# Window attention on one core: nine column pairs with nine tiles off ScalarE, and column heads staged in 128-channel tiles

## The chip, the cores and the metric

The kernel runs on one core of a Trainium2 chip. Each engine of the core takes its instructions in order: PE (TensorE) multiplies matrices into PSUM, ACT (ScalarE) computes exponentials, DVE (VectorE) and POOL (GpSimd) do elementwise work, and SP issues DMAs. The metric is the time of one execution on the device in microseconds (us). "Span" is the time between the first and the last instruction that the profiler saw.

## The reference

The input x is an image of 224 x 224 tokens with C = 96 channels. Half of the heads' channels (C2 = 48) attends within horizontal stripes of 8 rows, the other half within vertical stripes of 8 columns. A stripe has 8 x 224 = 1792 tokens.

```
qkv = einsum('bhwc,cd->bhwd', x, wqkv);  q, k, v = the three thirds
qh, kh, vh = the first 48 channels, as 28 row stripes of 1792 tokens
oh = softmax(qh @ kh^T * 48**-0.5) @ vh
qv, kv, vv = the last 48 channels, as 28 column stripes of 1792 tokens
ov = softmax(qv @ kv^T * 48**-0.5) @ vv
out = einsum('bhwc,cd->bhwd', concat(oh, ov), wo)
```

So there are 56 attention problems of 1792 x 1792 scores with 48 channels, and two projections around them. The row stripes give the first 48 channels of the concatenation ("row heads"), the column stripes the last 48 ("column heads").

## The kernel before, in words

**Pairs and tiles.** Two stripes are computed together as a pair P. Pairs 0 to 13 are row stripes, pairs 14 to 27 are column stripes (`ph_of`, L378; `NPH` is 14, `NP` is 28). The 1792 queries of a pair are cut into chunks of 512, 512, 512 and 256, the keys into 14 groups of 128. A score tile is 128 keys by 512 queries of both stripes, 128 x 1024 numbers in two PSUM banks; in the last chunk two key groups share a tile. A pair has 49 tiles (14 + 14 + 14 + 7).

**Three ways to an exponential.** Most tiles go to ACT: `qk_fn` (L682, matmuls at L689) fills one of two sets of score banks and `emit_qk` (L857) lets ACT write 2 to the power of the scores into a buffer PT (L859). The other tiles, listed in `KINDS` (L21) for each chunk of a pair, go around ACT as a polynomial on DVE and POOL (`emit_p`, L931, and `mids`, L953). A tile of kind P takes one DVE pass over the scores (L943), three POOL operations (L959, L960, L956), and a second set of scores that a second DVE pass (L948) combines with POOL's result. A tile of kind R has two DVE passes first (L943, L945), one POOL operation (L956) and the same closing pass. Both need their scores computed twice (`s_fn`, L695, matmuls at L702), into the ring of four PSUM banks (`RING`, L249). `KIND_OF` (L43) gives the kind of each pair: pair 0 has eight such tiles, pairs 1 to 13 nine, pairs 14 to 27 eight.

**From tile to output.** `pv_fn` (L708, L715) multiplies each finished tile with the values and adds up a chunk in one bank; `emit_ot` (L874) copies it to OT_sb. A DMA transpose (`turn_ot`, L420) puts tokens on partitions, DVE inverts the sums (`emit_rn`, L899), and POOL scales the rows (`emit_norm`, L909). Row heads are then copied by `keep_oh` (L427) into `cat`, which holds for every column stripe the 96 channels of its tokens; column heads are written into `cat` by POOL itself. When a column pair has both parts, `turn_cat` (L440) turns the pair's blocks of 96 channels with a DMA transpose into `oc_all`, packed without gaps: a block of tokens begins in one 128-row tile and may end in the next. `out_fills` (L623, matmuls at L637) multiplies them with `wo6`, which holds `wo` at the needed row offsets, one or two matmuls to each half of a block; DVE copies the result back into `cat` (L642), and each block of 128 tokens of one stripe is stored by one DMA (`emit_evict`, L879). The last pair is different: its row part goes through `out_fills` early, and at the end `fin_fills` (L585, L602) projects the column part straight from OT_sb, and DVE scales and adds it (L609, L614).

**What sets the order.** PE's order is written out by hand in `ORDER` (L44), one string for each pair. A letter is one step: q scores for ACT, v a PV step, 1 and 3 the first scores of a polynomial tile (in two halves or as one), 2 and 4 its closing scores, k the next of the projections for the following pair (`prep_fills`, L510), g the next head projection, f a step of `fin_fills`. From the letters a planner in the kernel's own program, with set durations for each kind of step, gives DVE, POOL and SP their orders (`dve_step`, `pool_step`, L996 and L1068). On the chip the orders are fixed and semaphores hold each instruction until its inputs are there. SP issues nearly all DMAs in one order: loads, transposes, copies and stores.

## Time and profile before

| | |
|---|---|
| median of 3 runs | 1062.62 us (1061.92 to 1063.65) |
| the profiled execution | 1062.68 us |
| its span | 1060.9 us |
| first exponential of a tile starts | 9.57 us |
| last exponential of a tile ends | 1055.97 us |
| granted PE clock, mean | 0.999 |

The page gives busy shares of each engine, then groups of instructions by source line: how many, their total and mean duration, and the idle time just before them with what ended it. A busy share counts overlapping instructions once. Stretches of the span are compared in a table by stage: pair 0 runs from 9.6 to 47.8 us, pairs 1 to 13 to 526.7, pair 14 to 565.2, pairs 15 to 26 to 1018.2, and pair 27 to 1056.0, each counted from its first exponential.

### The profile page before, as it was taken

What the parts mean: (1) busy time and instruction counts of PE and PEld (TensorE: products, weight loads), DVE (VectorE), ACT (ScalarE), POOL (GpSimd) and SP (SyncE); (2) the same over time, 40 slices, a digit from 0 to 9 for tenths busy, and PEclk for the clock granted to TensorE, in tenths of its full rate; (3) what the DMA queues carried; (4) which work ended last, traced back from release to release, by engine and by line L of the source; (5) the groups of instructions that cost most, each with busy time, mean ns of one, the idle gap of its engine ahead of it and who ended that gap; (6) DMA issues with size and microseconds to landing.
All of it is one profiled execution on the core that took longest, in us unless ns stands there. A gap on an engine that the chain in (4) does not pass through costs nothing.

```text
span 1060.9 us, 33547 instructions
## 1 busy us (share of the span) xinstructions
PE 1033.4 (97%) x13812; PEld 393.5 (37%) x13812; DVE 998.2 (94%) x1720; ACT 1049.3 (99%) x1146; POOL 935.5 (88%) x617
## 2 busy tenths in 40 slices
PE   9999999999999999999999999999999999999998
PEld 4333333333333333333334433333343443344433
DVE  8999999999999999999999999999999999999988
ACT  8999999999999999999999999999999999999998
POOL 7999999999988989999999778888888878979784
PEclk9999999999999999999999999999999999999999
DMA  9987648754963874322115334423332342332342
GB/s 182 160 153 112 100 80 145 112 96 84 144 96 56 139 108 69 38 56 58 40 20 99 76 54 76 88 38 77 80 69 52 81 83 49 79 79 40 64 65 44
DMA packets 376217, 88.58 MB, mean 83 GB/s; under 512 B 366944, under 2 KB 373376, under 8 KB 376064
## 3 DMA queue, kind: packets, MB, share of 16 engines
q1 hardware_dynamic: 374816, 85.85, 46.8%
q8 instruction: 108, 1.77, 0.7%
q10 hardware_dynamic: 1120, 0.49, 0.2%
q14 instruction: 45, 0.37, 0.1%
q0 software_dynamic: 128, 0.10, 0.0%
HBM read 28.36 MB, written 28.21 MB: 53 GB/s over the span
## 4 chain that ended last, share of the span: by engine, by line
PE 54%; ACT 28%; DVE 7%; issue 6%; POOL 4%; DMA 0%; ACTq 0%; POOLq 0%; DVEq 0%
ACT PT L859 28%; PE ps L715 20%; PE ps L689 20%; PE ps L702 7%; PE ps L521 3%; DVE qb L943 2%; DVE PT L948 2%; PE ps L637 2%; POOL PT L959 2%; PE ps L566 1%; POOL PT L956 1%; POOL PT L960 1%; DVE PT L945 1%; DVE KT_sb L526 1%; POOL cat L920 0%
## 5 line engine op out<-in xcount | busy, mean ns | idle before, releaser
L859 ACT ACTIVATE PT<-ps 128x1024 bf16<-128x1024 f32 x1135 | 1044.8, 1087 | 2.8 <-PE ps L689 1.8
L689 PE MATMUL ps<-QT_sb,KT_sb 49*64 49x512 bf16 (+1 forms) x5368 | 465.3, 363 | 17.6 <-ACT PT L859 10.5
L956 POOL TENSOR_TENSOR PT<-PT 128x1024 f16<-128x1024 f16 x237 | 445.1, 1892 | 41.1 <-DVE PT L945 24.1
L715 PE MATMUL ps<-PT,V_sb 128*49 128x512 bf16 (+1 forms) x3136 | 464.7, 362 | 0.3
L948 DVE SCALAR_TENSOR_TENSOR PT<-ps,PT 128x512 uint16<-128x512 f32 (+1 forms) x398 | 302.0, 787 | 20.8 <-PE ps L702 13.5
L943 DVE TENSOR_SCALAR qb<-ps 128x512 f16<-128x512 int16 (+1 forms) x404 | 302.3, 778 | 20.3 <-PE ps L702 15.8
L959 POOL TENSOR_TENSOR PT<-qb 128x1024 f16<-128x1024 f16 x141 | 266.1, 1892 | 54.8 <-DVE qb L943 24.9
L689 PEld LDWEIGHTS ps<-QT_sb,KT_sb 49*64 49x64 bf16 x5368 | 136.4, 103 | 305.8 <-ACT PT L859 280.9
L715 PEld LDWEIGHTS ps<-PT,V_sb 128*49 128x49 bf16 x3136 | 134.8, 103 | 211.1 <-issue 181.4
L702 PE MATMUL ps<-QT_sb,KT_sb 53*64 53x512 bf16 (+1 forms) x1896 | 189.4, 389 | 4.0 <-DVE PT L948 0.7
L960 POOL TENSOR_SCALAR PT<-PT 128x1024 f16<-128x1024 f16 x141 | 147.1, 1043 | 12.0
L945 DVE SCALAR_TENSOR_TENSOR PT<-ps,qb 128x512 f16<-128x512 int16 (+1 forms) x166 | 122.5, 766 | 0.5
L702 PEld LDWEIGHTS ps<-QT_sb,KT_sb 53*64 53x64 bf16 (+1 forms) x1896 | 53.8, 104 | 71.2 <-DVE PT L948 21.7
L876 DVE CAST OT_sb<-ps 113x512 bf16<-113x512 f32 x112 | 69.1, 617 | 3.0 <-PE ps L715 2.7
L535 DVE CAST QT_sb<-ps 128x512 bf16<-128x512 f32 (+1 forms) x111 | 67.2, 616 | 2.5 <-PE ps L521 1.7
L526 DVE TENSOR_SCALAR_CACHE_REDUCE KT_sb<-ps 128x512 bf16<-128x512 f32 x108 | 65.4, 616 | 1.3 <-PE ps L521 0.6
L642 DVE CAST cat<-ps 128x480 bf16<-128x480 f32 x84 | 51.5, 617 | 5.1 <-PE ps L637 4.5
L573 DVE CAST V_sb<-ps 128x480 bf16<-128x480 f32 (+1 forms) x84 | 51.7, 620 | 1.5 <-PE ps L566 1.2
L521 PE MATMUL ps<-xT_sb,w_sb 97*64 97x512 bf16 (+1 forms) x224 | 40.7, 364 | 0.0
L521 PE MATMUL ps<-xT_sb,wq_sb 97*64 97x512 bf16 x224 | 40.5, 366 | 0.1
L637 PE MATMUL ps<-wo,oc_all 128*64 128x96 bf16 x1176 | 39.9, 208 | 0.0
L566 PEld LDWEIGHTS ps<-w_sb,xT_sb 96*64 96x64 bf16 x1568 | 33.1, 112 | 17.7 <-issue 7.4
(64 smaller groups left out, 254.7 us busy)
## 6 DMA issues: line engine op xcount, KB each, us to landing
xT_sb<-xt_dram SPq DMA_DIRECT2D x28, 336.0 KB, 4.0
out_dram<-cat SPq DMA_DIRECT2D x382, 24.0 KB, 1.9
xp_dram<-in_x_dram SPq DMA_DIRECT2D x26, 336.0 KB
oc_all<-xp_dram SPq DMA_DIRECT2D x26, 336.0 KB, 4.4
xt_dram<-xT_sb SPq DMA_DIRECT2D x26, 336.0 KB, 6.4
cat<-ohn SPq DMA_DIRECT2D x52, 84.0 KB, 3.2
xt_dram<-xT_sb SPq DMA_DIRECT2D x4, 168.0 KB, 5.3
OT_tr<-OT_sb SPq DMA_TRANSPOSE x40, 3.4
```

The lines of the kernel that those rows point to most:

```text
L521: ins = e.matmul(bk[64 * w:64 * w + 64, 0:qs], lhsT=lw, rhs=xT_sb[b][0:C + 1, w, q0:q0 + qs], start=True, stop=True)
L526: return e.tensor_scalar(KT_sb[b][:, q0:q0 + qs], bk[:, 0:qs], alpha, None, ALU.mult, ALU.add, accum_out=ksum[b][:, c:c + 1])
L689: ins = e.matmul(bank(SETS[s] + w)[64 * kh:64 * kh + 64, i * t["qs"]:(i + 1) * t["qs"]], lhsT=KT_sb[b][64 * w:64 * w + CA, kt * 128 + 64 * ...
L702: ins = e.matmul(bank(bp[w])[64 * kh:64 * kh + 64, 0:512], lhsT=KT_sb[b][64 * w:64 * w + nr, kt * 128 + 64 * kh:kt * 128 + 64 * kh + 64], ...
L715: ins = e.matmul(bank(pb)[64 * w:64 * w + CA, 0:t["qs"]], lhsT=V_sb[b][:, w, kt, :], rhs=PT[slot][:, ca:ca + t["qs"]], start=st and i == 0 ...
L859: S.commit("act", 0.0, D_ACT, None, lambda e, s=s, slot=slot: e.activation(PT[slot][:], ps[:, 512 * SETS[s]:512 * SETS[s] + 1024], ACTF.Ex ...
L943: fn, reads, writes = lambda e: e.tensor_scalar(q, l, m, a, ALU.mult, ALU.add), bk, qk
L945: fn, reads, writes = lambda e: e.scalar_tensor_tensor(y.bitcast(FP16), l, -RA * 2.0 ** 16, q, ALU.add, ALU.mult), bk + qk, ptk
L948: fn, reads, writes = lambda e: e.scalar_tensor_tensor(y.bitcast(U16), f, 128.0, y.bitcast(FP16), ALU.mult, ALU.add), bk + ptk, ptk
L956: square = ("pool", D_SQ, lambda e: e.tensor_tensor(y, y, y, ALU.mult), yk + ["pser"], yk)
L959: return [("pool", D_SQ, lambda e: e.tensor_tensor(y, q, q, ALU.mult), qk, yk), ("pool", D_AF, lambda e: e.tensor_scalar(y, y, -(QS * (RB ...
L960: ("pool", D_AF, lambda e: e.tensor_scalar(y, y, -(QS * (RB + RA) / 2) ** 2, 1.0, ALU.add, ALU.mult), yk + ["pser"], yk),
```

## The change

- `KINDS` has a fourth kind with nine polynomial tiles (six P, three R), and nine of the column pairs have it: 15, 16, 17, 19, 20, 21, 23, 24 and 25. The other column pairs keep eight.
- Row heads are kept in `oh_all`. For a column pair, `rows_in` copies its row heads from there into one of two staging buffers `stg`, in which every block of tokens has 128 channels, 32 of them unused; POOL writes the column heads into the same buffer, and `turn_cat` turns it. A block of tokens then lies in one 128-row tile. Every half block takes one matmul, with one copy of `wo` in place of six. The copy is issued when the pair's first scores are; for pairs 27 and 14 it is issued in two parts, at the end of pairs 12 and 13's row work.
- The two turns of a pair no longer wait for each other through the old input buffer, and DVE's copies of the projection go into `og` and no longer back into `cat`, so they don't wait for the turns either.
- A block of the projection now holds 128 tokens, every partition two neighbouring ones: the weights are loaded with a step of two elements (`c (t u) -> c u t`), and one store carries two blocks, 384 bytes from each partition.
- The clearing of the unused channels (`stgz`) stands with the first memsets of the kernel; before, two smaller memsets stood in `later`.
- `do_fill2` and `emit_both` let one DVE instruction copy two neighbouring banks of a projection (letters K and G). The new `ORDER` has one K and no G.
- `ORDER` is new for pairs 0 to 4 and 11 to 27, and unchanged for pairs 6 to 10; that of pair 5 begins differently. Some of the planner's durations are new.

```diff
-KINDS = ["PPR PPR PP ", "PPR PRR PPR ", "PPR PPR PR "]
+KINDS = ["PPR PPR PP ", "PPR PRR PPR ", "PPR PPR PR ", "PPR PPR PPR "]
...
+KIND_OF = [0, 1, 1, 1, 1, 1, 1, 1, 1, 1, 1, 1, 1, 1, 2, 3, 3, 3, 2, 3, 3, 3, 2, 3, 3, 3, 2, 2]
 ORDER = [
...
-    "qv1qvvqvvvqgvqv2qvvq1vqgq3vqvkq3qvkqvvqkvvq4vqvkvq2vqgvq2qkvvqvvkq2qgvvq1qvv3qvkqvqvkqv4qgvvq3qvvvvq4qvvgq1qvv2qvqkvqvkkkqqvvv",
...
+    "vv1qvq4vqvkqvkq1vqgvqvvqv4qvvkq2qvvq1vvkqv1qkvq2qvvkqvgvq2qvvgvq1qvvgqvvvqv1qvqkq4gqvgvq3qvkq4qvvgq1qkvqvvkqvqvkgqv2qvq2vqvkvv",
...
-        cat = sb("cat", [128, NPH, NPH, 2, C], BF16)
+        oh_all = sb("oh_all", [128, NPH, NPH, 2, C2], BF16)
+        stg = [sb(f"stg{i}", [128, NKT, 2, 128], BF16) for i in range(2)]
+        og = [sb(f"og{i}", [128, NKT // 2, 2, 2, C], BF16) for i in range(3)]
         OT_tr = [sb(f"OT_tr{i}", [128, NKT, 128], BF16) for i in range(2)]
         ohn = sb("ohn", [128, NKT, 2, C2], BF16)
         rn = [sb(f"rn{i}", [128, 2 * NKT], FP32) for i in range(2)]
-        wo6 = sb("wo6", [128, 6, C], BF16)
-
-        x0_sb = cat[0:TH].rearrange("p a m w c -> p (a m w c)")[:, 0:2 * NTH * C].rearrange(
+        wo6 = sb("wo6", [128, C], BF16)
+
+        x0_sb = oh_all[0:TH].rearrange("p a m w c -> p (a m w c)")[:, 0:2 * NTH * C].rearrange(
             "p (w k c) -> p w k c", w=2, k=NTH)
-        NQT = 2 * NKT * C // 128
+        NQT = 2 * NKT
...
-            pool_now([("cat", NPH - 1)], lambda e: e.memset(cat[:, NPH - 1, :, :, C2:C].rearrange("p m w c -> p (m w) c").bitcast(FP32), 0.0), 0.7)
-            pool_now(["wo6z"], lambda e: e.memset(wo6[:].rearrange("p v c -> p (v c)").bitcast(FP32), 0.0), 0.3)
+        pool_now([("stgz", 0)], lambda e: e.memset(stg[0][:, :, :, C:].rearrange("p m w c -> p (m w) c").bitcast(FP32), 0.0), 0.5)
+        pool_now([("stgz", 1)], lambda e: e.memset(stg[1][:, :, :, :].rearrange("p m w c -> p (m w c)").bitcast(FP32), 0.0), 1.8)
...
-        def turn(semn, reads, writes, out_ap, in_ap):
-            d = {k for k in S.deps("dma", reads, writes) if k[0] != semn}
+        def turn(semn, reads, writes, out_ap, in_ap, old=()):
+            d = {k for k in S.deps("dma", reads, writes + list(old)) if k[0] != semn}
...
-                        dma("sp", [("ohn", 0), ("ohn", 1)], ["oh"], cat[64 * w:64 * w + 64, :, P, s_, 0:C2], src, "nc", tot)
+                        dma("sp", [("ohn", 0), ("ohn", 1)], ["oh"], oh_all[64 * w:64 * w + 64, :, P, s_, :], src, "nc", tot)
+
+        def rows_in(P, m0=0, m1=NPH):
+            b = P % 2
+            dma("sp", ["oh", ("stgz", b)], [("sr", b)], stg[b][:, m0:m1, :, 0:C2].rearrange("p m w c -> p (m w) c"),
+                oh_all[:, P - NPH, m0:m1, :, :].rearrange("p m w c -> p (m w) c"), f"ri{b}")
 
         def turn_cat(P, z):
-            b, a = P % 2, P - NPH
+            b = P % 2
             k0, k1 = ((0, 8), (8, NKT))[z]
-            flat = cat[:, a, :, :, :].rearrange("p m w c -> p (m w c)")
             x_old = [("x", w) for w in range(2)] if P in (NPH, NP - 1) else []
-            turn(f"oc{b}{z}", ["oh", ("cat", a), ("ov", a, z)], [("ocT", b, z), ("catd", a, z)] + x_old,
-                 oc_T[b][:, k0 * 2 * C // 128:k1 * 2 * C // 128, :], flat[:, k0 * 2 * C:k1 * 2 * C])
+            turn(f"oc{b}{z}", [("sr", b), ("sc", b, z), ("stgz", b)], [("ocT", b, z)],
+                 oc_T[b][:, 2 * k0:2 * k1, :], stg[b][:, k0:k1, :, :].rearrange("p m w c -> p (m w c)"), x_old)
 
         def load_wo():
-            for r0, n, p0, v in ((0, 96, 0, 0), (0, 32, 96, 1), (32, 64, 0, 2), (0, 64, 64, 3), (64, 32, 0, 4), (0, 96, 32, 5)):
-                dma("sp", ["wo6z"], ["wo6"], wo6[p0:p0 + n, v, :], wo[r0:r0 + n, :], "w2", 96)
+            dma("sp", [], ["wo6"], wo6[0:C, :], wo[:, :], "w2", 16)
...
-        dst_all = out[0].rearrange("(kt hh) (j dw) c -> j kt hh dw c", hh=16, dw=8)
+        dst_all = out[0].rearrange("(kp hh) (j dw) c -> j kp hh (dw c)", hh=32, dw=8)
...
-                                    t0 = (k0 + s) * 128 + 64 * h
+                                    t0 = (k0 + h) * 128
                                     ins = e.matmul(bk3[64 * h:64 * h + 64, s, :],
-                                                   lhsT=OT_sb[b][64 * w:64 * w + CA, t0:t0 + 64],
+                                                   lhsT=OT_sb[b][64 * w:64 * w + CA, t0:t0 + 128].rearrange("c (t u) -> c u t", u=2)[:, s, :],
...
-                            def d2(e, bk, s=s, ri=ri, w=w, kt=k0 + s, j=j):
+                            def d2(e, bk, s=s, ri=ri, w=w, kp=k0 // 2):
                                 bk3 = bk[:, 0:FS * (C + 1)].rearrange("p (s c) -> p s c", s=FS)
-                                return e.scalar_tensor_tensor(cat[:, NPH - 1, kt, w, :], bk3[:, s, 0:C], rc[ri][:, s:s + 1],
-                                                              cat[:, NPH - 1, kt, w, :], ALU.mult, ALU.add)
+                                return e.scalar_tensor_tensor(og[2][:, kp, w, s, :], bk3[:, s, 0:C], rc[ri][:, s:s + 1],
+                                                              og[2][:, kp, w, s, :], ALU.mult, ALU.add)
                             chain.append((0.225, d2, [("rc", ri), "add"], [("o", P, w, k0 + s)], None,
-                                          [(P, w, k0 + s)]))
+                                          [(P, w, k0 // 2, [("o", P, w, k0 + z) for z in range(n)])] if s == n - 1 else []))
...
-            rows = cat[:, a, :, :, :].rearrange("p m w c -> p (m w) c")
+            rows = og[2 if P == NP - 1 else b][:, :, :, :, :].rearrange("p m w s c -> p (m w s) c")
...
-                        q, r = divmod(3 * (k0 + s), 4)
-                        use = {0: ((0, 0),), 3: ((0, 1), (1, 2)), 2: ((0, 3), (1, 4)), 1: ((0, 5),)}[r]
-                        for i, (dq_, v) in enumerate(use):
-                            for h in range(2):
-                                ins = e.matmul(bk[64 * h:64 * h + 64, s * C:(s + 1) * C], lhsT=oc_T[b][:, q + dq_, 64 * h:64 * h + 64],
-                                               rhs=wo6[:, v, :], start=i == 0, stop=i == len(use) - 1)
+                        m, u = divmod(k0 + s, 2)
+                        for h in range(2):
+                            ins = e.matmul(bk[64 * h:64 * h + 64, s * C:(s + 1) * C],
+                                           lhsT=oc_T[b][0:C, 4 * (m // 2) + 2 * h + m % 2, :].rearrange("c (t u) -> c u t", u=2)[:, u, :],
+                                           rhs=wo6[0:C, :], start=True, stop=True)
                     return ins
 
                 def d(e, bk, k0=k0, n=n):
                     return e.tensor_copy(rows[:, k0:k0 + n, :], bk[:, 0:n * C].rearrange("p (s c) -> p s c", s=n))
                 last = P == NP - 1
-                st = [] if last else [(P, (k0 + s) % 2, (k0 + s) // 2) for s in range(n)]
-                fills.append(fill("B", 0.063 * n, pe_fn, ["wo6"] + [("ocT", b, y) for y in range(z + 1)],
-                                  [(0.07 + 96 * n * 0.001026, d, [("catd", a, y) for y in range(z + 1)], ["add"] if last else [("o", P, k0)], None, st)],
+                st = [] if last else [(P, m % 2, m // 2, sorted({("og", b, 2 * m // FS * FS), ("og", b, k0)})) for m in range(k0 // 2, (k0 + n) // 2)]
+                fills.append(fill("B", D_G * n, pe_fn, ["wo6"] + [("ocT", b, y) for y in range(z + 1)],
+                                  [(0.07 + 96 * n * 0.001026, d, [], ["add"] if last else [("og", b, k0)], None, st)],
...
-                    P, w, kt = item
-                    key = ("o", P, w, kt) if P == NP - 1 else st[3][0]
-                    dma(q, [key], [], dst_all[2 * (P - NPH) + w, kt], cat[:, P - NPH, kt, w, :], "op" if q == "gq" else f"out{P % 2}")
+                    P, w, kp, keys = item
+                    dma(q, keys, [], dst_all[2 * (P - NPH) + w, kp],
+                        og[2 if P == NP - 1 else P % 2][:, kp, w, :, :].rearrange("p s c -> p (s c)"), "op" if q == "gq" else f"out{P % 2}")
+
+        def emit_both(f1, f2, b0, done):
+            g, h = f1["gives"], f2["gives"]
+            P, b = g[1], g[1] % 2
+            if g[0] in "KQ":
+                q0, n = CH_Q0[g[2]], CH_SIZES[g[2]] + CH_SIZES[h[2]]
+                src = ps[:, 512 * b0:512 * b0 + n]
+                if g[0] == "K":
+                    def fn(e):
+                        return e.tensor_scalar(KT_sb[b][:, q0:q0 + n], src, alpha, None, ALU.mult, ALU.add,
+                                               accum_out=ksum[b][:, k_i[P, g[2]]:k_i[P, g[2]] + 1])
+                else:
+                    def fn(e):
+                        return e.tensor_copy(QT_sb[b][:, q0:q0 + n], src)
...
+            sts = [f1["chain"][0], f2["chain"][0]]
+            d = sts[0][0] + sts[1][0] - D_M2
+            S.commit("dve", 0.0, d, d + SEMD, fn, [("bank", b0), ("bank", b0 + 1)] + sorted(set(sts[0][2] + sts[1][2]), key=str), sts[0][3] + sts[1][3])
+            for st in sts:
...
-                    dst = cat[:, P - NPH, k0:k1, :, C2:C].rearrange("p m w c -> p (m w) c")
+                    dst = stg[b][:, k0:k1, :, C2:C].rearrange("p m w c -> p (m w) c")
...
-                            tm["sp"] += 3.5 + 5.3
-                            for y in range(2):
-                                turn_cat(NP - 1, y)
-                                g_t[NP - 1, y] = tm["sp"] + TURN
+                            rows_in(NP - 1, NPH - 1)
+                            rows_in(NPH, NPH - 1)
+                            tm["sp"] += 7.5
+                            turn_cat(NP - 1, 1)
+                            g_t[NP - 1, 1] = tm["sp"] + TURN
+                        elif P == NPH - 2:
+                            rows_in(NP - 1, 0, NPH - 1)
+                            rows_in(NPH, 0, NPH - 1)
+                            tm["sp"] += 10.4
+                            turn_cat(NP - 1, 0)
+                            g_t[NP - 1, 0] = tm["sp"] + TURN
...
-                    tm["sp"] = max(tm["sp"], st) + 1.5
+                    tm["sp"] = max(tm["sp"], st) + (4.0 if P > NPH else 3.2)
+                    if P > NPH:
+                        rows_in(P)
...
-                do_fill(c)
+                do_fill2(c.lower()) if c in "KG" else do_fill(c)
```

132 lines of the change are left out of this document (95 added, 37 removed).

## The prediction

> **What bounds the kernel now.** I read the page's busy shares first, then the costliest groups, then the busy time by stage, then who ACT waited for.
>
> ```profile
> span 1060.9 us, 33547 instructions
> PE 1033.4 (97%) x13812; PEld 393.5 (37%) x13812; DVE 998.2 (94%) x1720; ACT 1049.3 (99%) x1146; POOL 935.5 (88%) x617
> ...
> L859 ACT ACTIVATE PT<-ps 128x1024 bf16<-128x1024 f32 x1135 | 1044.8, 1087 | 2.8 <-PE ps L689 1.8
> ```
>
> Four engines stand above 88%, so a share alone does not say which one is the limit. The group row does: 1135 exponentials fill 1044.8 us with 2.8 us of idle before them.
>
> The next fence is the busy time by stage. Its columns are the stretch, its length, then PE, weight loads, DVE, ACT and POOL with the instructions in brackets. The rows are pair 0, pairs 1 to 13 (row heads, nine tiles each off ACT), two of those pairs on their own, pair 14, pairs 15 to 26 (column heads, eight tiles), and pair 27. Instructions that straddle an edge are counted in both stretches, so I count exponentials by KINDS: 41 where eight of the 49 tiles of a pair go elsewhere, 40 where nine do.
>
> ```profile
> 9.60:47.80 38.20, 36.76 (x522) 13.11 (x520) 36.62 (x66) 38.00 (x41) 34.26 (x22) 1.00 1.02 166
> 47.80:526.70 478.90, 465.84 (x5828) 167.43 (x5824) 461.10 (x774) 478.34 (x522) 446.02 (x293) 1.00 0.58 94
> 195.60:269.40 73.80, 72.01 (x900) 25.30 (x898) 71.98 (x121) 73.78 (x81) 71.90 (x46) 1.00 0.66 108
> 526.70:565.20 38.50, 37.78 (x481) 13.61 (x480) 36.41 (x64) 38.02 (x43) 37.56 (x25) 1.00 0.26 52
> 565.20:1018.20 453.00, 447.33 (x6402) 178.64 (x6400) 423.01 (x703) 452.65 (x493) 384.27 (x239) 1.00 0.36 69
> 1018.20:1056.00 37.80, 36.71 (x514) 14.65 (x510) 33.47 (x78) 37.77 (x42) 25.87 (x19) 1.00 0.27 52
> ```
>
> Per exponential that is 478.90/(13x40) = 0.921 us with row heads and 453.00/(12x41) = 0.921 us with column heads. The spacing is the same whether nine tiles go elsewhere or eight, while POOL's share is 93% in one and 85% in the other. So time is the number of exponentials times 0.921 us, wherever the other engines follow. Two places are slower: pair 14 (0.939 us) and pair 0 (0.932 us).
>
> ```profile
> ACT PT L859 <- PE ps L689: 1.8, 3, 1.2
> ACT PT L859 <- DVE PT L945: 0.3, 1, 0.3
> ```
>
> ACT's own waits come to 2.1 us, so the path is ACT, and PE answers each freed score bank just in time.
>
> **The change, part by part.**
>
> *Nine pairs with nine tiles.* KIND_OF gives kind 3 to nine column pairs, so 9 exponentials go (1135 to 1126, as the letter q counts in the two order lists). On ACT: 9 x 0.921 = 8.3 us less. In their place come nine tiles of kind P on PE, DVE and POOL. The rows are POOL's groups over the whole run, two DVE groups of pairs 15 to 26, and one line of the timeline.
>
> ```profile
> L956 POOL TENSOR_TENSOR PT<-PT 128x1024 f16<-128x1024 f16 x237 | 445.1, 1892 | 41.1 <-DVE PT L945 24.1 <-DVE wq_sb L552 7.5 <-PE ps L715 0.7
> L959 POOL TENSOR_TENSOR PT<-qb 128x1024 f16<-128x1024 f16 x141 | 266.1, 1892 | 54.8 <-DVE qb L943 24.9 <-ACT PT L859 8.9 <-PE ps L702 7.2
> L960 POOL TENSOR_SCALAR PT<-PT 128x1024 f16<-128x1024 f16 x141 | 147.1, 1043 | 12.0
> ...
> L943 DVE TENSOR_SCALAR qb<-ps 128x512 f16<-128x512 int16 x113 | 73.5, 683 | 5.4 <-PE ps L702 4.4
> L943 DVE TENSOR_SCALAR qb<-ps 128x1024 f16<-128x1024 int16 x39 | 47.6, 1221 | 6.2 <-PE ps L702 5.6
> ...
> 1047.07 1.29 DVE L948 SCALAR_TENSOR_TENSOR PT<-ps,PT 128x512 uint16<-128x512 f32 x2 [0.17 <-PE ps L702]
> ```
>
> POOL: 1.892 + 1.043 + 1.892 = 4.83 us a tile, 43.4 us for nine. DVE: two steps of 1.22 us (one wide) to 1.29 us (two halves), so 2.5 us a tile and 22.5 us in all. All nine tiles lie in pairs 15 to 25, so I set them against pairs 15 to 26: those will take (12x41 - 9) x 0.921 = 444.8 us. POOL: 384.27 + 43.4 = 427.7 us, 96%. DVE: 423.01 + 22.5 = 445.5 us, 100% as busy time counts. That overstates DVE, because a second half behind a first costs only 1.29 - 0.68 = 0.61 us, while the 113 halves of the row above fill 73.5 us, 0.65 each; that is 6% to be had by packing, up to 27 us over all of DVE. The two-pair row near 200 us shows that such a load can be carried: DVE 71.98 and POOL 71.90 of 73.80 us, 97% each, and ACT spaced 73.80/80 = 0.9225 us. I charge the nine pairs that spacing: 9 x 40 x 0.0015 = 0.5 us. The bound below is nothing; the bound above is pair 14's 0.939 us, the worst stretch here with POOL at 37.56 of 38.50: 9 x 40 x 0.018 = 6.5 us. I take 0.5, since the long row is the nearer load.
>
> *128-channel tiles for the column heads.* A head's block then needs two matmuls where three were the mean (1176 over 14 pairs x 28 blocks). The rows are the group and two places of the timeline.
>
> ```profile
> L637 PE MATMUL ps<-wo,oc_all 128*64 128x96 bf16 x1176 | 39.9, 208 | 0.0
> ...
> 605.34 0.69 PEld L637 LDWEIGHTS ps<-wo,oc_all 128*64 128x64 bf16 x30 [0.23 <-issue]
> ...
> 1037.66 0.41 PE L702 MATMUL ps<-QT_sb,KT_sb 53*64 53x512 bf16 x4
> 1037.90 0.39 PE L689 MATMUL ps<-QT_sb,KT_sb 49*64 49x512 bf16 x4
> 1038.22 0.49 PE L637 MATMUL ps<-wo,oc_all 128*64 128x96 bf16 x14
> 1038.64 0.41 PE L689 MATMUL ps<-QT_sb,KT_sb 49*64 49x512 bf16 x4
> 1038.98 0.62 PE L715 MATMUL ps<-PT,V_sb 128*49 128x512 bf16 x4
> ```
>
> Thirty weight loads start over 0.69 - 0.11 = 0.58 us, 20 ns each. So 392 matmuls fewer give PE 7.8 us. The last rows are starts on PE: score step to score step 0.24 us, score step to the other mode 0.34 us, so a change of mode costs 0.10. In pairs 14 to 27 the new list has 11 steps more (1760 against 1749) and 47 changes of mode fewer (959 against 1006). PE: -7.8 + 11 x 0.24 - 47 x 0.10 = -9.9 us. None of it is on the path, where ACT sets the pace; it is what makes room for the nine tiles.
>
> The remaining matmuls, and the last pair's at L602, load weights with a step of two elements (c u t). No row shows such a load. From below it costs nothing; from above twice the 20 ns, 784 x 20 = 15.7 us, which would make PE 5.8 us dearer than now. I take nothing, as the row whose count and width it shares. [...] No run here shows a stepped load yet.
>
> *Staging, turns, stores.* These go through SP's queue. The rows are three lines of the DMA issues (the last number is the median time to landing), the issue times of stores and turns on SP (shortest, median, longest ns), the turns' time to landing, and one turn in the timeline.
>
> ```profile
> out_dram<-cat SPq DMA_DIRECT2D x382, 24.0 KB, 1.9
> ...
> cat<-ohn SPq DMA_DIRECT2D x52, 84.0 KB, 3.2
> ...
> cat<-ohn SPq DMA_DIRECT2D x8, 42.0 KB, 2.2
> ...
> L287 SPq DMA_DIRECT2D out_dram<-cat x382: 538/598/1897, 594.5 to 1058.0; - x191
> ...
> L414 SPq DMA_TRANSPOSE oc_all<-cat x28: 1282/1434/2536, 560.3 to 1031.3; - x28
> ...
> DMA to landing us min/median/max: 3.2/4.5/6.0
> ...
> 1031.34 1.39 SPq L414 DMA_TRANSPOSE oc_all<-cat  x1
> ```
>
> Stores: 392 issues become 196. At 0.6 us each SP gains 118 us, or nothing if an issue of two blocks takes twice as long; either way SP is a waiter and no engine waits for a store before the last. rows_in adds one 336 KB copy a pair in 96-byte pieces. The nearest rows are the 84 and 42 KB copies of such pieces: 1.0 us for 42 KB more, so 2.2 + 7 x 1.0 = 9.2 us to landing, and no less than the 3.2 us of a quarter of it. It is issued when the pair's first scores are, ahead of both its turns, and the first turn waits in any case for the pair's first two chunks, 28 of its 49 PV steps: some 20 us. Hidden. A turn carries 16 and 12 tiles for 12 and 9: 1.43 to 1.9 us of issue, landing 4.5 to at most 6.0, or 6.0 to 8.0 if all of it scales. The tightest turn now is issued at 1031.34 and its first matmul starts at 1038.22, 6.9 us later. In the order lists the least distance from the last PV of a chunk to its first G grows from 21 to 23 exponentials for the first part and from 20 to 25 for the second, 1.8 and 4.6 us. So PE does not come to wait; cost nothing.
>
> *Start and end*, from the timeline.
>
> ```profile
> 1.40 1.59 POOL L331 MEMSET xT_sb<- 1x1792 f32 x1 [0.32 <-DVE ident L327]
> ...
> 8.83 0.69 POOL L362 MEMSET wqT<- 128x256 bf16 x2
> 12.81 3.74 POOL L959 TENSOR_TENSOR PT<-qb 128x1024 f16<-128x1024 f16 x2 [3.29 <-DVE qb L943]
> ...
> 1058.53 0.53 POOL L287 DMA_DIRECT2D out_dram<-cat  x1 [2.41 <-DVE cat L614]
> ```
>
> The two memsets of stg now run ahead of POOL's first tile: 1.6 us for 1792 words (stg1) and some 0.5 for a quarter of that. POOL idles 3.29 us there, so they are covered; without that cover they would push POOL's first tiles by 2.1 us, not ACT. At the end the last store is issued at 1058.53, after the last sum, and the span ends 2.4 us later. It still is one store after one sum, so the tail stays. The one paired K eviction saves DVE about 0.06 us.
>
> **The sum.** 1062.68 us is the profiled execution (span 1060.9 and 1.8 around it), 0.06 over the median of 1062.62. 1062.68 - 8.3 + 0.5 = 1054.9 us.
>
> **The rivals.**
>
> *A. The nine tiles overload POOL (slower).* POOL at 427.7 of 444.8 us leaves 17.1 us, 1.4 us a pair, for its waits on DVE and on its own results. The static order makes PE wait at the closing score step of a late tile, and the next scores stand behind that step. In pairs 1 to 13 POOL idled (478.90 - 446.02)/13 = 2.5 us a pair, in the two heavy pairs 0.95. At 2.5 the twelve pairs take 427.7 + 30 = 458 us instead of 444.8, and the run 1054.4 + 13.2 = 1067.6 us. The break-even with before is (444.8 + 8.3 - 427.7)/12 = 2.1 us a pair. For it: POOL's waits on L943 and L945 above. Against: that idleness was had where nothing pressed POOL. DVE at its limit would look the same.
>
> *B. Half of it.* POOL or DVE idles some 1.75 us a pair: 427.7 + 21 = 448.7, 3.9 us over, 1058.3 us.
>
> *C. Stepped weight loads are slow.* PE becomes 5.8 us dearer in a stage where it is busy 447.33 of 453.00 us, so up to 5.8 us go on the path: 1060.2 us. [...]
>
> *D. The order repairs pairs 0 and 14.* Both get new lists. At 0.921 us they would take 37.8 us each, 0.4 and 0.7 us less: 1053.8 us; and down to 1051.5 if spacing falls by 0.002 throughout.
>
> **How the numbers follow.** Forecast 0.60, D 0.12, B 0.10, C 0.07, A 0.11. The range 1051.5 to 1060.5 goes from D's floor to just past C and the worst case of the nine pairs (1054.4 + 6.5 = 1060.9), and leaves out A. A change within 0.2% (2.1 us) is about what a measurement of this kernel cannot tell from none. B and C are still faster by more than that, but C with the 6.5 us on top would be no change. So faster 0.85, same 0.04, slower 0.11.
>
> **What would show it.** Right: 1126 exponentials at 0.921 us or a little over in pairs 15 to 26, POOL and DVE each at 95% or more there, 784 matmuls in the head projection at 20 ns, ACT's waits still near 2 us. Wrong: spacing above 0.935 with the closing score steps waiting for POOL (A), weight loads of the projection above 20 ns apart (C), or PE waiting for a turn.

## The result and the profile after

The changed kernel takes 1056.15 us (median of 6 runs, 1055.85 to 1058.0), the kernel before 1062.34 us in the runs beside them. The ratio is 0.9944, 95% interval 0.9932 to 0.9957. The forecast was 1054.9 us with a range of 1051.5 to 1060.5 and most of the chance on "faster". The profiled execution is one of the longer ones, 1057.54 us with a span of 1055.7; the sum below is made against it.

The head of the page and the row of the exponentials:

```profile
span 1055.7 us, 32757 instructions
PE 1027.3 (97%) x13456; PEld 385.9 (37%) x13456; DVE 1014.0 (96%) x1748; ACT 1041.8 (99%) x1137; POOL 985.1 (93%) x654
...
L867 ACT ACTIVATE PT<-ps 128x1024 bf16<-128x1024 f32 x1126 | 1037.2, 1080 | 4.1 <-PE ps L697 2.9
```

Nine exponentials are gone and 356 matmuls. ACT is still the engine that is never free: 1126 exponentials fill 1037.2 us with 4.1 us of idle before them. The busy time by stage, cut where a pair's first exponential starts, with the columns as before: pair 0, pairs 1 to 13, pair 14, pairs 15 to 26, pair 27.

```profile
10.70:48.30 37.60, 36.67 (x522) 13.15 (x516) 35.82 (x59) 37.58 (x41) 34.54 (x24) 1.00 0.98 175
48.30:527.00 478.70, 465.95 (x5830) 166.04 (x5824) 461.12 (x772) 478.32 (x522) 448.71 (x293) 1.00 0.50 93
527.00:565.70 38.70, 38.52 (x504) 14.53 (x502) 37.72 (x66) 38.24 (x43) 36.92 (x23) 1.00 0.72 83
565.70:1011.90 446.20, 438.33 (x6002) 169.84 (x5998) 434.03 (x735) 445.18 (x485) 421.28 (x264) 1.00 0.51 83
1011.90:1049.80 37.90, 37.51 (x530) 15.81 (x528) 36.92 (x79) 37.87 (x42) 32.84 (x27) 1.00 0.49 81
```

Pairs 15 to 26 went from 453.00 to 446.20 us; every other stage stayed within 0.7 us of its time before. The five stretches together are 7.3 us shorter (1046.4 to 1039.1 us), and 6.8 of these lie there. Per exponential the stage stands at 446.20/483 = 0.924 us (0.921 before).

ACT's own waits for scores (in total, times, longest; the longest stands ahead of the first exponential, so only 0.6 us lie behind it), and the end of the span, from the timeline (start, length, then the instruction; in brackets the idle time before it):

```profile
ACT PT L867 <- PE ps L697: 2.9, 4, 2.3
```

```profile
1051.49 0.97 DVE L623 SCALAR_TENSOR_TENSOR og<-ps,rc,og 128x96 bf16<-128x96 f32 x4
1051.79 0.55 POOL L291 DMA_DIRECT2D out_dram<-og  x1 [0.67 <-DVE og L623]
1052.53 1.09 POOL L291 DMA_DIRECT2D out_dram<-og  x2 [0.19 <-DVE og L623]
```

The last exponential ends at 1049.81, the last sum at 1052.46. Then two stores, each of two blocks, are issued one after the other on POOL's queue, 1.09 us for both. Before, one store followed the last sum. The span ends 5.9 us after the last exponential, 4.9 before.

The new transfers, from the DMA issues (size, then median us to landing) and from the issue times of turns and stores on SP (shortest, median, longest ns). The line of landing times covers all DMAs that read or write `oc_all`; its longest, 7.9, is a turn:

```profile
out_dram<-og SPq DMA_DIRECT2D x181, 48.0 KB, 2.0
...
stg<-oh_all SPq DMA_DIRECT2D x13, 336.0 KB, 6.0
...
oc_all<-stg SPq DMA_TRANSPOSE x28, 4.4
```

```profile
L418 SPq DMA_TRANSPOSE oc_all<-stg x28: 1427/1887/4453, 539.6 to 1035.1; - x28
...
DMA to landing us min/median/max: 3.1/4.0/7.9
```

```profile
L291 SPq DMA_DIRECT2D out_dram<-og x181: 538/601/1592, 594.4 to 1049.9; - x181
```

A store of 384 bytes a partition costs SP the same 0.60 us as one of 192 did (medians), the copy of the row heads lands in 6.0 us and a turn in 4.4, at most 7.9. In pairs 15 to 26 PE waited for no DMA.

### The profile page after: what moved, and what is told of

Its sections match the earlier page's. It is cut to its first block, busy times and chain, and to the rows that moved or that the text cites. A ratio compares the mean times of both kernels' runs of the same rounds, so it can differ in the third digit from the quotient of the medians.

```text
span 1055.7 us, 32757 instructions
## 1 busy us (share of the span) xinstructions
PE 1027.3 (97%) x13456; PEld 385.9 (37%) x13456; DVE 1014.0 (96%) x1748; ACT 1041.8 (99%) x1137; POOL 985.1 (93%) x654
## 4 chain that ended last, share of the span: by engine, by line
PE 54%; ACT 22%; DVE 10%; POOL 7%; issue 6%; DMA 0%; ACTq 0%; POOLq 0%; DVEq 0%
ACT PT L867 22%; PE ps L723 20%; PE ps L697 20%; PE ps L710 7%; DVE PT L994 3%; POOL PT L1002 3%; PE ps L530 3%; DVE qb L989 3%; POOL PT L1005 2%; PE ps L575 1%; POOL PT L1006 1%; PE ps L644 1%; DVE PT L991 1%; DVE og L650 1%; DVE V_sb L582 1%
## 5 line engine op out<-in xcount | busy, mean ns | idle before, releaser
L867 ACT ACTIVATE PT<-ps 128x1024 bf16<-128x1024 f32 x1126 | 1037.2, 1080 | 4.1 <-PE ps L697 2.9
L1002 POOL TENSOR_TENSOR PT<-PT 128x1024 f16<-128x1024 f16 x246 | 461.8, 1894 | 20.3 <-DVE PT L991 11.3
L994 DVE SCALAR_TENSOR_TENSOR PT<-ps,PT 128x512 uint16<-128x512 f32 (+1 forms) x405 | 312.4, 799 | 15.7 <-PE ps L710 6.8
L989 DVE TENSOR_SCALAR qb<-ps 128x512 f16<-128x512 int16 (+1 forms) x421 | 313.7, 775 | 11.9 <-PE ps L710 7.8
L1005 POOL TENSOR_TENSOR PT<-qb 128x1024 f16<-128x1024 f16 x150 | 283.2, 1894 | 22.9 <-DVE qb L989 10.8
L710 PE MATMUL ps<-QT_sb,KT_sb 50*64 50x512 bf16 (+1 forms) x1968 | 196.6, 390 | 5.3 <-DVE PT L994 1.2
L1006 POOL TENSOR_SCALAR PT<-PT 128x1024 f16<-128x1024 f16 x150 | 156.9, 1046 | 12.8
L710 PEld LDWEIGHTS ps<-QT_sb,KT_sb 50*64 50x64 bf16 (+1 forms) x1968 | 55.8, 103 | 76.3 <-DVE PT L994 22.9
L650 DVE CAST og<-ps 128x480 bf16<-128x480 f32 x84 | 51.4, 617 | 1.4 <-PE ps L644 0.7
L530 PE MATMUL ps<-xT_sb,w_sb 97*64 97x512 bf16 x224 | 41.9, 371 | 0.3 <-DVE qb L989 0.2
L575 PE MATMUL ps<-w_sb,xT_sb 96*64 96x48 bf16 x1568 | 39.1, 190 | 0.0
```

The source lines that it names most:

```text
L530: ins = e.matmul(bk[64 * w:64 * w + 64, 0:qs], lhsT=lw, rhs=xT_sb[b][0:C + 1, w, q0:q0 + qs], start=True, stop=True)
L575: ins = e.matmul(bk[64 * h:64 * h + 64, j * C2:(j + 1) * C2], lhsT=xT_sb[b][0:C, w, t0:t0 + 64], rhs=w_sb[0:C, wblk(P, "v"), 0:C2], start= ...
L710: ins = e.matmul(bank(bp[w])[64 * kh:64 * kh + 64, 0:512], lhsT=KT_sb[b][64 * w:64 * w + nr, kt * 128 + 64 * kh:kt * 128 + 64 * kh + 64], ...
L867: S.commit("act", 0.0, D_ACT, None, lambda e, s=s, slot=slot: e.activation(PT[slot][:], ps[:, 512 * SETS[s]:512 * SETS[s] + 1024], ACTF.Ex ...
L989: fn, reads, writes = lambda e: e.tensor_scalar(q, l, m, a, ALU.mult, ALU.add), bk, qk
L994: fn, reads, writes = lambda e: e.scalar_tensor_tensor(y.bitcast(U16), f, 128.0, y.bitcast(FP16), ALU.mult, ALU.add), bk + ptk, ptk
```

## The experiments

Times of stages in this part are worked out from the rows of the exponentials, as in the tables by stage. "Stretch" is the time from the first exponential's start to the last one's end: 1046.4 us before, 1039.1 in the profile after.

### The parts without the nine tiles, and the nine tiles without the parts

The first kernel is the changed one with the lists of the kernel before, the second the kernel before with the new lists (one K written as kk).

```diff
-KINDS = ["PPR PPR PP ", "PPR PRR PPR ", "PPR PPR PR ", "PPR PPR PPR "]
+KINDS = ["PPR PPR PP ", "PPR PRR PPR ", "PPR PPR PR "]
-KIND_OF = [0, 1, 1, 1, 1, 1, 1, 1, 1, 1, 1, 1, 1, 1, 2, 3, 3, 3, 2, 3, 3, 3, 2, 3, 3, 3, 2, 2]
+KIND_OF = [0, 1, 1, 1, 1, 1, 1, 1, 1, 1, 1, 1, 1, 1, 2, 2, 2, 2, 2, 2, 2, 2, 2, 2, 2, 2, 2, 2]
 ORDER = [
...
```

> The changed kernel with the kinds and the order list of before: staging in 128-channel tiles, rows copied ahead, stores of two blocks, but 1135 exponentials. Theory (the time is the number of exponentials times 0.921 us, the other parts only make room): as before, 1061 to 1064 us, ACT spacing 0.921 us, although the head projection has 392 matmuls fewer. Rival (the relief of PE and SP is itself worth the gain): 1056 to 1059 us.

Measured: 1064.28 us, ratio 1.0015 [1.0006, 1.0025], just above the range that was expected. The stage of pairs 15 to 26:

```profile
566.00:1019.90 453.90, 444.10 (x6044) 170.89 (x6042) 422.42 (x703) 452.77 (x493) 384.21 (x239) 1.00 0.53 84
```

It took 453.9 us (453.0 before) and the stretch 1047.0 (1046.4). So staging, free turns, stores of two blocks and two matmuls in place of three bring nothing by themselves, although PE's busy time in the stage fell from 447.3 to 444.1 us.

```diff
-KIND_OF = [0, 1, 1, 1, 1, 1, 1, 1, 1, 1, 1, 1, 1, 1, 2, 2, 2, 2, 2, 2, 2, 2, 2, 2, 2, 2, 2, 2]
+KIND_OF = [0, 1, 1, 1, 1, 1, 1, 1, 1, 1, 1, 1, 1, 1, 2, 3, 3, 3, 2, 3, 3, 3, 2, 3, 3, 3, 2, 2]
 ORDER = [
...
```

> The kernel before with the new kinds and the new order list (its one letter K written as two k): 1126 exponentials, but three matmuls to a block, the old staging and a store for each block. Theory (room on PE is needed for the nine tiles): part of the 8.3 us is lost, 1057 to 1061 us, with spacing in pairs 15 to 26 above 0.924 us. Rival (ACT's count alone decides, PE had room enough): 1055 to 1057 us, as the changed kernel.

Measured: 1072.8 us, ratio 1.0102 [1.0084, 1.012], a loss and outside both expectations. Three prices come out of its trace against that of the changed kernel. Pair 14 took 44.9 us instead of 38.7; its timeline shows why:

```profile
561.66 5.00 SPq L414 DMA_TRANSPOSE oc_all<-cat  x2
...
565.41 0.77 PE L637 MATMUL ps<-wo,oc_all 128*64 128x96 bf16 x14 [4.07 <-DMA oc_all<-cat]
...
567.72 1.02 ACT L859 ACTIVATE PT<-ps 128x1024 bf16<-128x1024 f32 x1 [5.55 <-PE ps L689]
```

The new order asks for the projection of pair 27's row part earlier than before, and without the row heads staged ahead its turn is issued only at 561.66; in the changed kernel that turn goes out at 539.57. PE stands 4.07 us, ACT 5.55, and PE's granted clock is at half from 563.12 to 569.95 us (more of that below). Pairs 15 to 26 took 451.9 us instead of 446.2, though the same tiles were on POOL and DVE:

```profile
571.40:1023.40 452.00, 443.45 (x6344) 175.01 (x6343) 433.87 (x734) 448.75 (x484) 416.88 (x260) 1.00 0.35 66
```

PE has 342 matmuls more in it (6344 against 6002). The run with repeated matmuls below puts a price of 3.4 us on 268; what makes the rest of these 5.7 us isn't shown. And the tail was 9.6 us, with single-block stores still queued:

```profile
1057.74 11.84 SPq L287 DMA_DIRECT2D out_dram<-cat  x17
...
1060.84 7.16 ACTq L287 DMA_DIRECT2D out_dram<-cat  x11
```

So the nine tiles give the gain and the parts make it possible: neither does anything useful alone. This holds for the new lists, which were made for the new parts; lists with nine tiles made for the old parts were not run.

### Is the rest POOL's, DVE's or PE's?

The stage ended 0.9 us above the forecast of 445.3. Three kernels take work away from an engine by leaving out columns of the polynomial tiles. One more kernel adds work to PE.

POOL: the affine step on half of the columns.

```diff
-lambda e: e.tensor_scalar(y, y, -(QS * (RB + RA) / 2) ** 2, 1.0, ALU.add, ALU.mult)
+lambda e: e.tensor_scalar(y[:, 0:512], y[:, 0:512], -(QS * (RB + RA) / 2) ** 2, 1.0, ALU.add, ALU.mult)
```

> The changed kernel, with POOL's middle operation on half of its columns (left out: the affine step on the other half of each polynomial tile of kind P), all orders unchanged: POOL has about 0.5 us less in each of 150 tiles. If POOL's lateness makes the stalls of the nine-tile pairs (rival A of the prediction): ACT's stretch from first to last exponential falls from 1039 to 1036 us or less. If not: it stays within 1 us of 1039.

Measured: 1055.67 us, ratio 0.9935 [0.992, 0.995]. POOL's work in pairs 15 to 26 fell from 421.3 to 392.5 us, the stage took 446.3 us and the stretch 1038.8.

```profile
563.60:1009.90 446.30, 438.17 (x6002) 169.59 (x5998) 433.26 (x734) 445.27 (x485) 392.45 (x263) 1.00 0.51 83
```

Nothing came of 28.8 us less, so POOL's lateness makes none of the remaining stalls.

DVE: the closing pass on half of its columns.

```diff
+                if h == 2:
+                    f, y = f[:, :, 0:256], y[:, :, 0:256]
+                else:
+                    f, y = f[:, 0:256], y[:, 0:256]
                 fn, reads, writes = lambda e: e.scalar_tensor_tensor(
```

> The changed kernel, with DVE's closing pass on half of its columns (left out: the exponent of the other half), all orders unchanged: DVE has about 0.5 us less in each of 246 tiles. If DVE's lateness makes the stalls: ACT's stretch falls from 1039 to 1035 us or less, near 1126 x 0.917 = 1032.5. If not: it stays within 1 us of 1039.

Measured: 1055.19 us, ratio 0.9929 [0.9912, 0.9946]; the stage 445.5, the stretch 1037.5. 46.4 us less work on DVE (434.0 to 387.6) bought 0.7 us in the stage and 1.6 in the stretch, between the two outcomes that were expected.

PE and DVE: that kernel with the closing scores on half of their columns too.

```diff
+            nc_ = 512 if nr == 50 else 256
...
-bank(bp[w])[64 * kh:64 * kh + 64, 0:512],
+bank(bp[w])[64 * kh:64 * kh + 64, 0:nc_],
...
-rhs=QT_sb[b][64 * w:64 * w + nr, t["q0"]:t["q0"] + 512], start=True, stop=True)
+rhs=QT_sb[b][64 * w:64 * w + nr, t["q0"]:t["q0"] + nc_], start=True, stop=True)
```

> The run with DVE's closing pass halved, and PE's closing scores halved with it (256 of 512 columns; left out: the other half of those scores), orders unchanged: PE has some 0.1 us less in each of 246 tiles. If what is left of the stalls is PE's: ACT's stretch falls from 1037.5 us to 1035.5 or less. If it is ACT's own or the order's latencies: within 0.7 us of 1037.5.

Measured: 1054.14 us, ratio 0.9916 [0.9901, 0.9932]; the stage 445.0, the stretch 1036.9.

```profile
563.60:1008.60 445.00, 431.13 (x6002) 166.60 (x5998) 386.15 (x736) 444.82 (x484) 421.42 (x264) 1.00 0.52 83
```

PE was busy 431.1 us instead of 437.0 and the stage gained 0.5 us. ACT is busy in 444.82 of these 445.00 us, so what is left of the spacing (445.0/483 = 0.921 us) is ACT's own pace.

PE the other way: some blocks of the head projection are multiplied twice. The edit repeats every second block of a step, and a step has five blocks or three, so two of five and one of three: 308 matmuls more, and not the 392 that the expectation counts.

```diff
-                        for h in range(2):
+                        for h in (0, 1, 0, 1) if s % 2 else (0, 1):
```

> The changed kernel with every second block of the head projection multiplied twice into the same place, so that it has the 1176 matmuls of before and 7.8 us more of PE work, orders unchanged. If that room on PE is needed by the nine tiles: pairs 15 to 26 take 450 to 452 us in place of 446.2 and the time is 1060 to 1062 us, by the run without the parts. If it is hidden as in the kernel before: 446 to 447 us, and the time 1056 to 1057 us.

Measured: 1060.7 us (10 runs), ratio 0.9977 [0.9968, 0.9986]. The stage:

```profile
565.40:1015.00 449.60, 442.32 (x6270) 174.08 (x6266) 433.98 (x735) 447.17 (x485) 421.62 (x264) 1.00 0.52 82
```

The projection's matmuls in that run, 784 in the changed kernel (shortest, median, longest ns):

```profile
L644 PE MATMUL ps<-wo,oc_all x1092: 202/206/233, 561.3 to 1052.9; 96*64 96x96 bf16 x182
```

268 of the 308 lie in the stage (6270 against 6002). At the prediction's 20 ns they are 5.4 us of work; PE's busy time grew by 4.0 us (438.33 to 442.32). The stage grew by 3.4 us, the stretch by 3.6. So PE is near its edge: taking 5.9 us away gained 0.5, adding 4.0 to 5.4 cost 3.4. The nine tiles have used up most of the relief from two matmuls in place of three.

### Is POOL at its edge too?

Ahead of POOL's affine step stands a memset of a buffer that nothing reads.

```diff
+        dump = [sb(f"dump{i}", [128, 256], BF16) for i in range(6)]
...
-("pool", D_AF, lambda e: e.tensor_scalar(y, y, -(QS * (RB + RA) / 2) ** 2, 1.0, ALU.add, ALU.mult), yk + ["pser"], yk),
+("pool", D_AF, lambda e, dp=dump[tl["no"] % 6]: (e.memset(dp[:], 0.0), e.tensor_scalar(y, y, -(QS * (RB + RA) / 2) ** 2, 1.0, ALU.add, ALU.mult))[1], yk + ["pser"], yk),
```

> The changed kernel with a memset of 128 x 256 bf16 (about 0.3 us) ahead of POOL's middle operation in each of 150 tiles, orders unchanged: 69 such tiles lie in pairs 15 to 26, so 21 us more on POOL there, past what ACT's 446 us leave. If POOL is next in line (the threshold of rival A): pairs 15 to 26 take 450 us or more and the time is 1060 us or more. If the waits of POOL give the room: 446 to 448 us and 1056 to 1058 us.

Measured: 1084.66 us, ratio 1.0197 [1.0182, 1.0211]. The stage took 462.4 us, 16.2 more, for 21.1 us more POOL work. The stage, and four of the largest waits that concern the polynomial tiles, over the whole run (us in total, times, longest):

```profile
572.70:1035.10 462.40, 448.29 (x6002) 171.21 (x6000) 434.69 (x734) 447.55 (x484) 442.35 (x333) 0.97 0.50 80
```

```profile
PEld ps L711 <- DVE PT L995: 35.5, 87, 2.2
ACT PT L868 <- PE ps L698: 21.4, 32, 1.8
...
DVE PT L995 <- POOL PT L1003: 13.2, 11, 2.4
PE ps L711 <- DVE PT L995: 10.8, 16, 1.9
```

That is rival A's chain: DVE waits for POOL, PE for DVE at the closing scores, ACT for PE. But the row has a second reading. The granted clock in it is 0.97, and the extra time sits in four pairs: 15, 17, 21 and 26 took 41.2, 40.5, 41.8 and 41.2 us, 15.0 of the 16.2 us together. Each of them holds a stretch at half clock. The windows around the first one, cut on the grid of 3.41 us on which the clock changed in this trace (the second number after the length is PE's busy time, the third number from the end the granted clock):

```profile
571.29:574.70 3.41, 3.41 (x50) 1.33 (x42) 2.38 (x4) 3.41 (x5) 3.41 (x2) 1.00 1.13 143
574.70:578.11 3.41, 2.29 (x24) 0.69 (x22) 3.05 (x7) 2.50 (x3) 3.41 (x3) 1.00 0.84 99
578.11:581.53 3.42, 3.42 (x30) 0.95 (x26) 2.85 (x6) 2.38 (x3) 3.23 (x5) 0.50 1.23 176
581.53:584.94 3.41, 3.41 (x28) 0.85 (x28) 1.58 (x2) 2.05 (x2) 3.33 (x3) 0.50 0.53 107
584.94:588.36 3.42, 3.27 (x44) 0.97 (x36) 3.09 (x9) 3.21 (x4) 3.42 (x3) 1.00 0.00 0
```

PE was busy for 2.29 of 3.41 us, and for the next two such windows it ran at half speed. So two theories stood: POOL's work is the price, or the price is the clock, which POOL's lateness only brings down. A smaller memset, 128x64, tells them apart.

```diff
-        dump = [sb(f"dump{i}", [128, 256], BF16) for i in range(6)]
+        dump = [sb(f"dump{i}", [128, 64], BF16) for i in range(6)]
```

> POOL's added memset shrinks from 128x256 to 128x64. The larger one took 313 ns; I estimate 0.16 us, so 69 x 0.16 = 11 us more POOL work in pairs 15 to 26, half of the 21.1 us of the run before. In that run pairs 15 to 26 took 16.2 us longer, but four of them also held stretches at half the granted clock (6.8, 3.4, 10.2 and 3.4 us, 23.9 us together), each one right after a stretch of 3.41 us in which PE was busy for 2.3 us or less. Theory 1, POOL's work is the price: with about 5 us of room the stage grows by 11 - 5 = 6 us, to 452 us, and the run to about 1064 to 1066 us. Theory 2, the price is the clock, which POOL's lateness only releases: PE's stretches stay above 2.3 us of 3.41, the granted clock stays full to the end, the stage grows by at most 2.5 us, to 448.7, and the run to at most 1059.5 us.

Measured: 1063.19 us median of 10 runs, ratio 1.0006 [0.9995, 1.0017], and from 1061.45 to 1067.84 us. The profiled run (1061.61 us) kept the full clock:

```profile
566.60:1015.70 449.10, 439.14 (x6002) 169.90 (x5998) 433.79 (x734) 446.17 (x485) 430.38 (x332) 1.00 0.51 83
```

Neither theory had it alone. With the clock full, 68 x 0.152 = 10.3 us of POOL work lengthened the stage by 2.8 us, close to the second theory's 2.5, and the stretch by 5.3. Of the other 2.5 us, 2.2 lie in pairs 1 to 13, whose tiles have the memset too and which the 1059.5 us of the second theory left out. The run with the larger memset says the same there: the clock was full in pairs 1 to 13, and 65 x 0.312 = 20.3 us of POOL work lengthened them by 7.0 us (478.6 to 485.7). So POOL's work has a price without the clock. The timed median is higher still than the profiled run, and the mean granted clock of those runs goes with the time: 1.000 at 1061.45 us, 0.998 at 1063.11, 0.996 at 1064.10, 0.992 at 1067.84. So POOL has little room: between a fifth and a third of the added work comes out at once, and past that late tiles also went with a lower clock, 0.97 over the stage with the larger memset. By the pairs of numbers above a lower clock makes some 6 us of the longest run with the smaller one, of which no trace is left.

The same for DVE: a memset of 128x128 ahead of each tile's last closing pass.

```diff
+        dump = [sb(f"dump{i}", [128, 128], BF16) for i in range(14)]
+        turns = [0]
...
-                fn, reads, writes = lambda e: e.scalar_tensor_tensor(
-                    y.bitcast(U16), f, 128.0, y.bitcast(FP16), ALU.mult, ALU.add), bk + ptk, ptk
+                def fn(e):
+                    if h:
+                        turns[0] += 1
+                        e.memset(dump[turns[0] % 14][:], 0.0)
+                    return e.scalar_tensor_tensor(y.bitcast(U16), f, 128.0, y.bitcast(FP16), ALU.mult, ALU.add)
+                reads, writes = bk + ptk, ptk
```

> DVE gets a memset of 128x128 bf16 ahead of each closing pass, one a tile. A DVE memset of 64 words of 128 partitions took 112 ns at the start of the kernel, so 105 x 0.112 = 11.8 us more in pairs 15 to 26, where DVE is busy 434.0 of 446.2 us: 445.8, nothing left. If DVE is at its edge the stage grows by most of that, 6 to 11 us, and the run to 1062 to 1070 us. If busy time overstates DVE, as the prediction has it (a half behind a half costs 0.61 us and is counted with 0.65), the stage grows by at most 3 us and the run to at most 1060 us. Making DVE's closing passes lighter had shortened the stage by 0.8 us.

Measured: 1055.62 us, ratio 0.9939 [0.9922, 0.9955].

```profile
563.40:1009.70 446.30, 438.41 (x6002) 170.12 (x5998) 434.33 (x837) 445.33 (x485) 421.08 (x264) 1.00 0.51 83
```

102 memsets more of 112 ns each are in the row, 11.4 us, and DVE's busy time is 434.33 us, 0.3 more than without them, because 93% of the memsets' time overlaps the passes around them. They aren't free for that: where one half of a closing pass follows the other, their starts lie 682 ns apart in the median with a memset between them and 608 without, so a memset takes 74 ns of DVE's time, and 102 of them 7.5 us. The stage is 0.1 us longer. DVE at 97% is not full; POOL at 94% nearly is.

### The tail

Two durations of the planner, changed so that the last stores go out over three queues (ACT 3, POOL 3, SP 17) and not mostly over POOL (1, 14, 8).

```diff
-D_ST, D_SW, D_TAIL = 1.0, 0.60, 1.0
+D_ST, D_SW, D_TAIL = 1.0, 1.3, 0.70
```

> The changed kernel with the planner's two store costs of before (1.3 and 0.70 us in place of 0.60 and 1.0), which moves eleven of the last stores from POOL's queue to SP's and ACT's; nothing else moves. If the longer end (5.9 us after the last exponential, 4.9 before) comes from the last two stores going one after the other on POOL's queue: the end is 5.2 to 5.4 us and the time 0.5 to 0.7 us less. If it comes from the later last sum or the larger store: no change in the end.

Measured: 1054.92 us, ratio 0.9927 [0.9915, 0.994], tail 5.1 us instead of 5.9. To see whether it beats the changed kernel, both were timed again on one chip.

> The changed kernel as it is, on one chip with the next run. Its time should again be 0.994 of the kernel before. If the time of the first exponential hangs on when PE's clock reaches full speed, as it seems over the profiles so far (8.8 us where the clock is full at 4.7 us, 10.7 us where at 10.4), this profile's pair of numbers lies on the same line.

> The changed kernel with its last stores spread over SP's, ACT's and POOL's queues, beside the changed kernel on the same chip. By the end after the last exponential (5.08 against 5.87 us) it should take 0.8 us less; if the 1054.9 us of its first run was the chip or the clock's start, the two are within 0.3 us.

Measured: the changed kernel 1057.36 us, ratio 0.9947 [0.9934, 0.996]; the spread tail 1058.35, ratio 0.9954 [0.9941, 0.9968]: 1.0 us more where 0.8 less was expected. In the profiles the tail is again 5.1 against 5.9 us. The six timed runs of the spread tail go from 1055.12 us at a mean clock of 1.000 to 1060.61 at 0.996, those of the changed kernel from 1056.49 to 1057.6 at 0.999 and 1.000. The 0.8 us of the tail are real in the profiles and smaller than the scatter of the runs, which goes with the clock. Where the clock fell in those runs isn't known, since they left no trace. No version is shown to beat the changed kernel.

## Why the prediction was right, and where its terms were off

**The forecast's mechanism held.** The predicted time was 1.25 us below the median, and 2.6 below the profiled execution. The difference of the profiled execution, from the stages: the first exponential 1.15 us later (10.72 against 9.57), the tail 1.0 longer, pairs 15 to 26 0.9 over 445.3, pair 0 0.6 shorter, the others 0.1 together. Of the terms that the sum did not hold, pair 0's thus hides a part of the others. Of the signs of being right, the 1126 exponentials and the 20 ns came; POOL stood at 94% (421.28 of 446.20 us) where 95% or more was said, and DVE at 97%, with 434.03 us and not the 445.5 of the sum.

**Nine exponentials less.** 1126 of them, as foreseen. The term of 8.3 us minus 0.5 for spacing came out at 6.8. The mis-sized part is the spacing, 0.924 us over the stage in place of 0.9225 in nine pairs and 0.921 in three. Against 0.921 throughout (444.8 us) the stage is 1.4 us over; with DVE's and PE's work lightened 1.2 of it went, with POOL's none. It is not spread evenly: pairs 17 (37.4 us) and 26 (38.3), each 0.6 over, hold most of it, and pair 26 has eight tiles, not nine. The choice of the long row near 200 us over pair 14's as the nearer load was right: 0.5 was said, 1.4 measured, 6.5 the upper bound.

**Two matmuls in place of three.** PE fell by 9.0 us in pairs 15 to 26 (447.33 to 438.33), against -9.9 over all column pairs. "None of it is on the path" was right, by the kernel with the parts alone, which gained nothing. The prediction left out that the room is nearly all taken: 268 matmuls given back, 5.4 us at 20 ns each, cost 3.4 (repeated matmuls). The weight loads' share in that run, 174.08 of 449.60 us or 39%, does not tell how near PE is to its edge.

**Stepped weight loads.** Taken at nothing, which no row of before showed, and nothing it was: within a step of the projection the loads start 19.9 ns apart in the mean, 19.2 before (gaps over 0.2 us, where loads were taken ahead, left out), and the matmuls 20.7 ns apart, 21.1 before. Ten of the loads:

```profile
608.93 0.27 PEld L644 LDWEIGHTS ps<-wo,oc_all 96*64 96x64 bf16 x10 [0.23 <-issue]
```

The first starts 0.27 - 0.11 = 0.16 us before the last, 18 ns a load. Rival C is out: this step of two elements cost nothing that the trace shows.

**Staging and turns.** Landing 6.0 us (median) lies within the stated 3.2 to 9.2, the issue of a turn at 1.89 us (median, 4.45 at most) within 1.43 to 1.9, its landing at most 7.9 within 8.0. The row of landings that this started from, 3.2/4.5/6.0, holds all DMAs of `oc_all` and not the turns alone: these took 3.7 us in the median before and 5.8 at most, and 4.4 and 7.9 now. "PE does not come to wait" held. What the prediction did not see is the step's worth: it is costed at nothing because it is hidden, but with the old staging the new order loses 6.2 us in pair 14.

**"The tail stays" was wrong.** It was read from the last store alone. With two blocks to a store the planner put 14 of the last 23 stores on POOL, and two are issued after the last sum; the tail grew by 1.0 us. The run with the stores spread, where it grew by 0.2, shows that their order made 0.8 of it. No row of before shows the new order of the last stores, so the term needed a range and was given none.

**The start.** The sum has no term for it. In the profiled run the first exponential came 1.15 us later; over the traces its time goes with the clock (below). In the profile of the second set of runs the changed kernel starts it at 9.70 us.

**The rivals.** A did not happen, and its break-even was misplaced. It was put at 2.1 us of POOL idleness a pair; there were (446.20 - 421.28)/12 = 2.1 us, and the run was 6 us faster. The reason is POOL's work, which came to 421.28 us and not to 427.7: with it the break-even is (444.8 + 8.3 - 421.28)/12 = 2.65 us. Pair 27 has 7 us more of POOL's work than before (25.87 to 32.84). What A lacked is the clock: in the run with the larger memset a late tile cost its wait and then, after a window in which PE was busy for 2.29 us or less, 3.4 us or more at half speed. B's stage of 448.7 us did not come either. C with the 6.5 us on top was called no change, but its sum is 1060.2 + 6.5 - 0.5 = 1066.2 us, 3.5 us slower than before. Of D, pair 0 was repaired (37.6 us, 0.4 foreseen less than before, 0.6 measured) and pair 14 was not (38.7): PE is busy 38.52 of its 38.70 us there, which points to PE; no run tests it.

## What to carry to other kernels

Where one engine sets the pace, count what leaves it and then ask of every other engine what a little more work on it costs, by adding some: here 4.0 to 5.4 us on PE cost 3.4, 10.3 us on POOL 2.8 and 7.5 us on DVE next to nothing, which no busy share told (98%, 94%, 97%). Count what an edit really adds: the repeated matmuls were fewer than meant, and a memset's 112 ns took 74 of DVE's time. A step that brings nothing alone may carry another one, so undo parts both ways round. And look at the last instructions of each queue when the number of stores changes: the tail has its own order.
